# Second layer's attention weight gradients: keys' jobs first, their sets and factor loaded in the last blocks of the feed-forward gradient

## The chip, the cores and the metric

The kernel runs on one core of a Trainium2 chip. The metric is the device time of one execution in microseconds (us); lower is better. The core has five engines with a queue each: TensorE (PE, matmuls into PSUM), VectorE (DVE), ScalarE (ACT), GpSimd (POOL) and SyncE (SP), which here issues every DMA.

## What is computed

The reference runs four residual layers on 2048 tokens of width 512, two linear-attention layers (A) and two gated feed-forward layers (B), in the order A, B, A, B with shared weights, and returns the output and the gradients of the input and of the five weight matrices.

```python
def _fwd_reference(A_x, A_wqkv, A_wo, B_x, B_w_gate, B_w_up, B_w_down):
    def _A_ref(x, wqkv, wo):
        H = 32; Dh = D // H
        qkv = (x @ wqkv).reshape(B, S, 3, H, Dh) ...
        phi = lambda t: jnp.where(t > 0, t + 1, jnp.exp(t)) + 1e-6
        pq, pk = phi(q), phi(k)
        kv = jnp.einsum("bhsd,bhse->bhde", pk, v)
        z = jnp.einsum("bhsd->bhd", pk)
        num = jnp.einsum("bhqd,bhde->bhqe", pq, kv)
        den = jnp.einsum("bhqd,bhd->bhq", pq, z)[..., None] + 1e-6
        return (num / den) ... @ wo
    def _B_ref(x, w_gate, w_up, w_down):
        h = _sigmoid(x @ w_gate) * (x @ w_up)
        return h @ w_down
    x = A_x
    x = x + _A_ref(_layernorm(x), A_wqkv, A_wo)
    x = x + _B_ref(_layernorm(x), B_w_gate, B_w_up, B_w_down)
    x = x + _A_ref(_layernorm(x), A_wqkv, A_wo)
    x = x + _B_ref(_layernorm(x), B_w_gate, B_w_up, B_w_down)
    return x
...
_out, _vjp = jax.vjp(_f, A_x, A_wqkv, A_wo, B_w_gate, B_w_up, B_w_down)
```

Layers are numbered 0 to 3 in the code (A, B, A, B). The "second layer" of the title is layer 2, the second attention layer.

## The kernel before

The forward pass stores what the backward pass needs in device memory: the normalized inputs `sv_h`, for attention `sv_pk`, `sv_phq`, `sv_pqn`, for the feed-forward layers `sv_ssd`. The backward pass goes through layers 3, 2, 1, 0. The gradient of the residual stays in SBUF.

**Feed-forward gradient.** `BBwd.run` handles a B layer in four blocks B of 512 tokens, each in 11 steps u over 128 columns of the hidden width. `D(n)` multiplies the gradient by `wdT` (L1481, tile `dhh_ps`, PSUM tag "g" with two banks), ACT copies it to `dhb` (L1487), DVE and POOL multiply with the two halves of `ssd` into `dd` (L1488, L1489). `R(n)` closes a group of three columns: DVE transposes `dd` in 32 by 32 pieces into `tr_stg` (L1092; three buffers) and SP stores them as `sv_hdd` or, for the last group, `sv_hdl` (L1095). `H(B, u)` multiplies `dd` by `wuT` and `wgT` (L1513). `D` and `R` run two steps ahead of `H`. After a group's last `D` the group after next is loaded (`load_ssd`, L1461, two buffers), which the object keeps as `last_ssd`. A block ends with the layer norm's gradient, among it four operations on DVE (L1330) and ACT (L1311). `hooks` maps a place `(B, u)` to a function that is called there.

**Attention gradient.** `ABwd.first` goes through 16 row tiles `st`; for each there are TensorE's `dp_ps`, `gT_ps` and `dz_ps` and on DVE six operations (L1886, L1887, L1931, L1933, L1936, L1937). Then come `GT_ps` (L1987) and `ABwd.second`.

**Weight gradients.** These are made in `p2_gen`, a generator that is stepped between other work. One job makes a group of columns of one weight's gradient, from a set of two halves (`p_set`, two buffers each) and a factor with all 2048 tokens (`p_a` in the profile). A job has four units of 16 matmuls (L1807, `p_ps`, PSUM tag "u" with two banks), one for each 128 rows; each unit is evacuated to `dw_stg`, by ACT (L1824) if the sum over the two layers isn't finished yet and by DVE (L1822, adding the part stored before) if it is. `prefetch(i + 2)` in a job's last unit loads the set of the job after next into the buffers that this job has done with. The attention jobs are 256 columns wide. Their sets are of queries (`sv_dq`, two plain loads of 512 KB, L1673) or of keys (`sv_dkT`, four transposing loads of 256 KB, L1670), 1 MB each. Their factor is `sv_h` of the layer, loaded in four quarters of 512 KB (L1740).

**The second list of jobs, `w2`**, is opened by the hook `open_w2` at `(1, 0)` of layer 1's feed-forward gradient. It holds the four attention jobs of layer 2 in the order query, query, key, key (`a_jobs`), then twelve feed-forward jobs of layer 1 (the first is the last columns of `wd`, whose set is `sv_hdl`), then four attention jobs of layer 0. Opening it loads `MT` (`load_MT`, for the next attention gradient), the set of job 0, the factor and the set of job 1. Its units are consumed from the end of layer 1's block 3: two there, 20 in `ABwd.first` of layer 0 (one for each row tile and one more after each fourth), the rest later.

**Order of the work.** PE, ACT, DVE and POOL run in the order in which the code traces instructions (`manual_schedule(engines=EM)`). SP isn't in `EM`: a scheduler of the compiler orders its DMAs by its own estimate of when each is ready, those traced earlier first. So a load can go long before the place where the code has it, when its buffer is free; `tc.issue_after(ins)` puts what is traced in it behind `ins` on its queue.

```python
def prefetch(i):
    ...
    with k.tc.issue_after(R.pins.pop(i)) if i in R.pins else nullcontext():
        h = dict(set=(p2_set if nm == "wqkv" else p2_set_b)(k, R, *src))
```

Of the kernel before, what the change touches and what calls it, by code (L numbers as in the profile page):

```python
# [9 lines left out]
BF16 = mybir.dt.bfloat16  # L10
# [8 lines left out]
D = 512  # L19
# [3 lines left out]
P = 128  # L23
NST = S // P
# [7 lines left out]
NB = 4  # L32
GW = 256
# [32 lines left out]
def kernel(  # L66
# [22 lines left out]
    k = K()  # L89
# [20 lines left out]
    for l in range(4):  # L110
# [26 lines left out]
        wqkv=dram.tile([D, 2 * D], BF16, name="dwp_wqk"),  # L137
# [98 lines left out]
    if True:  # L236
        def load_b_weights(after):
            k.wdT = wb.tile([P, NDC, FP], BF16, name="wdT", tag="w_c")
            k.wuT = wb.tile([P, NFC, D], BF16, name="wuT", tag="w_a")
            k.wgT = wb.tile([P, NFC, D], BF16, name="wgT", tag="w_b")  # L240
            half = NFC // 2 + 1
            parts = [(k.wdT[:, c:c + 2, :], k.wT["wdT"][c * P:(c + 2) * P, :]) for c in (0, 2)]
            for t_sb, src in ((k.wuT, k.wT["wuT"]), (k.wgT, k.wT["wgT"])):
                parts += [(t_sb[:, c:e, :], src[c * P:e * P, :]) for c, e in ((0, half), (half, NFC))]
            for ins, (dst, src) in zip(after, parts):
                with tc.issue_after(ins):
                    nc.sync.dma_start(out=dst, in_=src.rearrange("(c p) j -> p c j", p=P))

        def load_MT(l):
            k.MT = k.mtp.tile([P, NDC, D], BF16, name="MT")  # L250
            nc.sync.dma_start(out=k.MT[:], in_=k.sv[l]["MT"].rearrange("(c p) j -> p c j", p=P))

        def load_a_weights(l):
            k.wqkvT = wb.tile([P, 3 * NDC, D], BF16, name="wqkvT", tag="w_a")
            woT_GT = wb.tile([P, 2, NDC, D], BF16, name="woT_GT", tag="w_b")
            k.Nv = wb.tile([P, NDC, D], BF16, name="Nv", tag="w_c")
            k.woT, k.GT = woT_GT[:, 0, :, :], woT_GT[:, 1, :, :]
            view = lambda d: d.rearrange("(c p) j -> p c j", p=P)
            yield nc.sync.dma_start(out=k.woT, in_=view(k.wT["woT"]))
            for i in (2, 0, 1):  # L260
                yield nc.sync.dma_start(out=k.wqkvT[:, i * NDC:(i + 1) * NDC, :],
                                        in_=view(k.wT["wqkvT"][i * D:(i + 1) * D, :]))
        k.load_b_weights, k.load_a_weights, k.load_MT = load_b_weights, load_a_weights, load_MT

        R = P2Res(k)
        w = {}

        def open_a1():
            k.pre["close"]()
            R.big = bctx.enter_context(tc.tile_pool(name="p2pool", bufs=1, side="right", reuse_waits="tile"))  # L270
            k.mtp = bctx.enter_context(tc.tile_pool(name="MTp", bufs=1, side="right", reuse_waits="tile"))
            k.load_MT(2)
            w["h3"] = b_load_all(k, R, k.sv[3]["h"], "p2_a1")

        def open_a2(l):
            k.a2ctx = ExitStack()
            pool = (k.a2ctx if l == 3 else bctx).enter_context(
                tc.tile_pool(name=f"a2_{l}", bufs=1, reuse_waits="tile"))

            k.a2 = pool.tile([P, NST, D], BF16, name="p2_a2")  # L280
            k.load_a2 = lambda b: b_load_batch(k, R, k.a2, k.sv[l]["gbf"], b)

        def open_sets():
            R.sets = bctx.enter_context(tc.tile_pool(name="p2sets", bufs=2, side="right", reuse_waits="tile"))
            R.stage = bctx.enter_context(tc.tile_pool(name="p2stage", bufs=2, side="right", reuse_waits="tile"))
            R.pins = dict(enumerate(B3.ssd_dmas[-2:]))
            w[3] = Units(p2_gen(k, R, b_jobs(k, 3, lambda: w["h3"])), b_units())
            return w[3]

        def open_w2():  # L290
            k.load_MT(0)
            jobs = a_jobs(k, 2, once(lambda: a_load_all(k, R, k.sv[2]["h"], "p2_a1")))
            jobs += b_jobs(k, 1, lambda: w["h1"]) + a_jobs(k, 0, lambda: w["h0"])
            w[2] = Units(p2_gen(k, R, jobs), len(jobs) * NDC)
            return w[2]

        def load_h1(b):
            if b == 0:
                w["h1"] = R.big.tile([P, NST, D], BF16, name="p2_a1")
            b_load_batch(k, R, w["h1"], k.sv[1]["h"], b)  # L300
        k.load_h1 = load_h1

        A2, A0 = ABwd(k, R, 2), ABwd(k, R, 0, out1)
        B3.run(A2, {(1, 8): open_a1, (3, 5): open_sets})
        open_a2(3)
        w3 = w[3]
        A2.first(w3)
        A2.second(w3)
        w3.take(w3.left - 4)
        k.a2ctx.close()  # L310
        BBwd(k, 1).run(A0, {(1, 0): open_w2}, rest=w3)
        open_a2(1)
        R.stage_a = bctx.enter_context(tc.tile_pool(name="p2stage_a", bufs=2, reuse_waits="tile"))
        w2 = w[2]
        A0.first(w2)
        A0.second(w2)
        tail = bctx.enter_context(tc.tile_pool(name="t_big", bufs=1, reuse_waits="tile"))
        last = 2 * D // GW * NDC
        w["h0"] = tail.tile([P, NST, D], BF16, name="t_a1")
        for b in range(NST // NB):  # L320
            w2.take(NDC)
            R.tail = tail
            with tc.issue_after(R.last_set):
                a_load_batch(k, R, w["h0"], k.sv[0]["h"], b)
        T = {}
        loads = a_small_loads(k, tail, T)
        for i in range(w2.left - last):
            next(w2)
            with tc.issue_after(R.last_set):
                next(loads, None)  # L330
        drain(loads)
        sg = a_small_grads(k, tail, T)
        for i in range(last):
            if i == last - 1:
                next(sg, None)
            next(w2)
            if i % 2 == 1 and i < last - 1:
                next(sg, None)
        drain(w2)
        drain(sg)  # L340
# [52 lines left out]
def dram_batch(ap2d, b, nb=NB):  # L393
    return ap2d[batch_rows(b, nb), :].rearrange("(n p) d -> p n d", p=P)
# [1236 lines left out]
def drain(gen):  # L1631
    for _ in gen:
        pass


class Units:

    def __init__(self, gen, n):
        self.gen, self.left = gen, n
        self.R = next(gen)  # L1640

    def __iter__(self):
        return self

# [9 lines left out]
def b_units():  # L1654
    return 3 * (NG + 1) * NDC
# [45 lines left out]
def b_jobs(k, l, h):  # L1701
    sv, nms, final = k.sv[l], ("wd", "wu", "wg"), l == 1
    wd = [(0, g) for g in range(NG + 1)]
    if final:
        order = wd[NG:] + wd[:NG] + [(i, g) for g in range(NG + 1) for i in (1, 2)]
    else:
        order = [(i, g) for g in (0, NG, 1) for i in (1, 2)] + [wd[g] for g in (0, NG, 1, 2)] + [(1, 2), (2, 2)]
    return [(nms[i], (sv, i, g), CG[g][0] * P, XG if g < NG else F - NG * XG, final, h if i else lambda: k.a2)
            for i, g in order]


def a_jobs(k, l, h):
    n = D // GW
    return [("wqkv", (k.sv[l], g // n, g % n), g * GW, GW, l == 0, h) for g in range(2 * n)]


def once(f):
    got = []

    def get():  # L1720
        if not got:
            got.append(f())
        return got[0]
    return get


def b_load_batch(k, R, t, src, b):
    R.eng().dma_start(out=t[:, b * NB:(b + 1) * NB, :].rearrange("p (n e) d -> p n e d", e=2),
                      in_=src[batch_rows(b), :].rearrange("(n p e) d -> p n e d", p=P, e=2))


def b_load_all(k, R, src, name, pool=None):
    t = (pool or R.big).tile([P, NST, D], BF16, name=name)
    for b in range(NST // NB):
        b_load_batch(k, R, t, src, b)
    return t


def a_load_batch(k, R, t, src, b):
    R.eng().dma_start(out=t[:, b * NB:(b + 1) * NB, :], in_=dram_batch(src, b))  # L1740


def a_load_all(k, R, src, name):
    t = R.big.tile([P, NST, D], BF16, name=name)
    for b in range(NST // NB):
        a_load_batch(k, R, t, src, b)
    return t


def p2_gen(k, R, jobs):  # L1750
# [41 lines left out]
        return [lambda j0=j0: part(j0) for j0 in range(0, n, 2)]  # L1792

    prefetch(0)
    jobs[0][5]()
    prefetch(1)
    yield R
    for i, (nm, src, c0, w, final, factor) in enumerate(jobs):
        h = held.pop(i)
        set_t = h["set"]  # L1800
# [422 lines left out]
```

## Time and profile before

| what | us |
|---|---|
| median of 3 runs | 1098.92 (1098.82 to 1100.64) |
| profiled execution | 1098.47 |
| its span, first to last instruction | 1096.8 |
| layer 1's feed-forward gradient, blocks 0 to 3 | about 709 to 824 in the span |
| layer 0's `ABwd.first`, row tiles with `w2` units | about 824 to 885 |
| layer 0's GT and `ABwd.second` | about 885 to 965 |
| remaining units of `w2` | about 965 to 1094 |

Busy shares of the span are TensorE 98%, VectorE 65%, ScalarE 44%, GpSimd 42%; the mean granted TensorE clock is 1.000. The DMA queue moved 268.81 MB, taking 86.5% of the 16 engines' span.

How to read the lines below: times within the span are in us from its start. In a waits row, the numbers are the total us waited, how often, and the longest. In a timeline row, they are start and duration in us, engine, line, operation, the tiles as out<-in, and, in brackets, idle time just before and what ended it. In a windows row each engine has its busy us and the number of its instructions in the stretch.

### The profile page before, as it was taken

What the parts mean: (1) busy time and instruction counts of PE and PEld (TensorE: products, weight loads), DVE (VectorE), ACT (ScalarE), POOL (GpSimd) and SP (SyncE); (2) the same over time, 40 slices, a digit from 0 to 9 for tenths busy, and PEclk for the clock granted to TensorE, in tenths of its full rate; (3) what the DMA queues carried; (4) which work ended last, traced back from release to release, by engine and by line L of the source; (5) the groups of instructions that cost most, each with busy time, mean ns of one, the idle gap of its engine ahead of it and who ended that gap; (6) DMA issues with size and microseconds to landing.
All of it is one profiled execution on the core that took longest, in us unless ns stands there. A gap on an engine that the chain in (4) does not pass through costs nothing. (4 is left out here: it accounts for less than half of the span.)

```text
span 1096.8 us, 19853 instructions
## 1 busy us (share of the span) xinstructions
PE 1076.1 (98%) x7239; PEld 660.6 (60%) x7340; DVE 718.2 (65%) x1257; ACT 483.2 (44%) x905; POOL 464.1 (42%) x631
## 2 busy tenths in 40 slices
PE   8999999999999999999999999999999999999998
PEld 4467777547777744445756556544447755555587
DVE  7798997878888677777965630067778946632221
ACT  6676555647555524445633441234346513420001
POOL 5738776425765447773101420048871102410000
PEclk9999999999999999999999999999999999999999
DMA  8948997895797688875899978998869999968997
GB/s 252 321 156 213 253 248 240 225 247 154 213 296 231 188 271 292 297 254 194 250 256 272 252 233 281 289 318 261 233 189 240 281 247 281 249 201 272 257 273 169
DMA packets 383202, 270.08 MB, mean 246 GB/s; under 512 B 134976, under 2 KB 368896, under 8 KB 383104
## 3 DMA queue, kind: packets, MB, share of 16 engines
q1 hardware_dynamic: 383104, 268.81, 86.5%
q8 instruction: 57, 0.93, 0.3%
q14 instruction: 41, 0.34, 0.1%
HBM read 122.62 MB, written 119.47 MB: 221 GB/s over the span
## 5 line engine op out<-in xcount | busy, mean ns | idle before, releaser
L1807 PE MATMUL p_ps<-p_set,p_a 128*128 128x384 bf16 (+2 forms) x1792 | 264.7, 303 | 2.0 <-DVE dw_stg L1822 0.7
L1807 PEld LDWEIGHTS <-p_a 128*128 128x128 bf16 x1792 | 168.8, 96 | 86.2 <-issue 2.0
L1489 POOL TENSOR_TENSOR dd<-dhb,ssd 128x512 bf16<-128x512 bf16 x84 | 96.9, 1158 | 101.5 <-ACT dhb L1487 94.3
L1488 DVE TENSOR_TENSOR dd<-dhh_ps,ssd 128x512 bf16<-128x512 f32 x85 | 57.2, 679 | 118.7 <-ACT dhb L1487 114.9
L1513 PE MATMUL dh_ps<-wuT,dd 128*128 128x512 bf16 (+1 forms) x339 | 128.5, 379 | 0.5
L1513 PE MATMUL dh_ps<-wgT,dd 128*128 128x512 bf16 (+1 forms) x329 | 124.7, 379 | 0.1
L1513 PEld LDWEIGHTS <-dd 128*128 128x128 bf16 x680 | 66.3, 98 | 79.8 <-POOL dd L1489 0.4
L1154 POOL TENSOR_TENSOR ssd_t<-hhT,oms 128x512 bf16<-128x512 bf16 (+2 forms) x76 | 83.9, 1112 | 45.6 <-DVE hhT L1153 18.2
L1822 DVE TENSOR_TENSOR dw_stg<-p_ps,dw_stg 128x384 bf16<-128x384 f32 (+2 forms) x76 | 32.0, 438 | 105.4 <-PE p_ps L1807 95.9
L1487 ACT CAST dhb<-dhh_ps 128x512 bf16<-128x512 f32 x84 | 48.7, 589 | 114.7 <-PE dhh_ps L1481 106.9
L1135 PE MATMUL g_ps<-hT,wg 128*128 128x256 bf16 (+1 forms) x792 | 92.8, 261 | 0.7 <-DVE den L974 0.4
L1135 PE MATMUL u_ps<-hT,wu 128*128 128x256 bf16 (+1 forms) x792 | 92.8, 261 | 0.0
L1092 DVE STREAM_TRANSPOSE tr_stg<-dd 128x768 f32<-128x768 f32 (+1 forms) x62 | 86.9, 1437 | 4.7 <-DMA sv_hdd<-tr_stg 3.6
L1135 PEld LDWEIGHTS <-wg 128*128 128x128 bf16 x792 | 70.0, 98 | 16.9 <-issue 0.5
L1170 PE MATMUL y_ps<-wd,hhT 128*128 128x512 bf16 (+1 forms) x337 | 77.9, 379 | 0.8
L1481 PE MATMUL dhh_ps<-gT,wdT 128*128 128x512 bf16 x299 | 76.7, 379 | 1.7 <-DVE dd L1488 0.9
L1135 PEld LDWEIGHTS <-wu 128*128 128x128 bf16 x792 | 70.6, 98 | 7.4 <-issue 0.4
L1151 ACT ACTIVATE ssd_t<-g_ps 128x512 bf16<-128x512 f32 (+2 forms) x76 | 42.5, 559 | 61.7 <-PE g_ps L1135 54.1
L1824 ACT CAST dw_stg<-p_ps 128x384 bf16<-128x384 f32 (+2 forms) x76 | 28.1, 386 | 85.3 <-PE p_ps L1807 81.5
L1481 PEld LDWEIGHTS <-wdT 128*128 128x128 bf16 x352 | 34.3, 98 | 42.5 <-issue 2.7
L1152 ACT ACTIVATE oms<-g_ps 128x512 bf16<-128x512 f32 (+2 forms) x96 | 53.7, 559 | 10.9 <-POOL ssd_t L1154 9.9
L1153 DVE TENSOR_TENSOR hhT<-u_ps,ssd_t 128x512 bf16<-128x512 f32 (+2 forms) x76 | 47.3, 630 | 16.8 <-PE u_ps L1135 9.1
(259 smaller groups left out, 1878.4 us busy)
## 6 DMA issues: line engine op xcount, KB each, us to landing
sv_hdd<-tr_stg SPq DMA_DIRECT2D x72, 384.0 KB, 4.7
p_set<-sv_hdd SPq DMA_DIRECT2D x36, 768.0 KB, 6.4
ssd<-sv_ssd SPq DMA_DIRECT2D x23, 768.0 KB, 5.2
sv_ssd<-ssd_t SPq DMA_DIRECT2D x61, 256.0 KB, 3.5
h_ld<-sv_h SPq DMA_DIRECT2D x30, 256.0 KB, 4.1
sv_hdl<-tr_stg SPq DMA_DIRECT2D x24, 256.0 KB, 4.8
p_a<-sv_h SPq DMA_DIRECT2D x12, 512.0 KB, 6.6
p_set<-sv_hdl SPq DMA_DIRECT2D x24, 256.0 KB, 4.7
```

The costliest lines, as they stand in the source:

```text
L1092: nc.vector.transpose(t[:, :, 0:n * P].bitcast(F32).rearrange("p q (a j) -> p q a j", a=2 * n), src.rearrange("p c x -> p (c x)").bitcast( ...
L1135: nc.tensor.matmul(ps[:, ci * n:(ci + 1) * n], lhsT=w_sb[:, kc, (c0 + ci) * P:(c0 + ci + 1) * P], rhs=hT[:, kc, (st % 2) * P:(st % 2) * P ...
L1152: nc.scalar.activation(oms, gv, ACT.Sigmoid, scale=-1.0)
L1153: nc.vector.tensor_tensor(hh, uv, ssd[:, :, 0, :], ALU.mult)
L1154: nc.gpsimd.tensor_tensor(ssd[:, :, 1, :], hh, oms, ALU.mult)
L1170: nc.tensor.matmul(y_ps[:], lhsT=h[0:r, fc, off:off + P], rhs=k.wd[0:r, fc, :], start=(fc == 0), stop=(fc == NFC - 1))
L1481: nc.tensor.matmul(ps[:], lhsT=k.wdT[:, jc, u * P:(u + 1) * P], rhs=self.gT[B][:, jc, :], start=(jc == 0), stop=(jc == NDC - 1))
L1487: nc.scalar.copy(dhb[:], ps[:])
L1488: nc.vector.tensor_tensor(self.dd[ng][:, 0, c, :], ps[:], self.ssd[ng][:, c, 0, :], ALU.mult)
L1489: nc.gpsimd.tensor_tensor(self.dd[ng][:, 1, c, :], dhb[:], self.ssd[ng][:, c, 1, :], ALU.mult)
L1513: nc.tensor.matmul(self.acc[j][:], lhsT=dd[0:r, a, c, j * P:(j + 1) * P], rhs=w[0:r, u, :], start=(u == 0 and a == 0), stop=(u == NFC - 1 ...
L1807: nc.tensor.matmul(ps[:, 0:w], lhsT=lhs[:, s, ic * P:(ic + 1) * P], rhs=rhs, start=(s == 0), stop=(s == NST - 1))
```

## The change

Two things are changed for `w2`. The four attention jobs of layer 2 come in the order key, key, query, query (groups 2, 3, 0, 1). And what `open_w2` loaded at once is spread over hooks in layer 1's feed-forward gradient: `MT` at `(1, 2)`; the four quarters of the factor at `(2, 1)`, `(2, 4)`, `(2, 7)` and `(2, 10)`; the first keys' set at `(3, 2)`, with the opening of the list; the second keys' set at `(3, 5)`. All but `MT` are put behind the latest `ssd` load on SP's queue. `p2_gen` now stops once after its first prefetch and once after its second; `Units.ahead` steps it from the one to the other, and the earlier list `w3` calls it right away. `w2` then loads its queries' sets by `prefetch(2)` and `prefetch(3)`.

```diff
             w[3] = Units(p2_gen(k, R, b_jobs(k, 3, lambda: w["h3"])), b_units())
+            w[3].ahead()
             return w[3]
 
+        def load_h2(b):
+            if b == 0:
+                w["h2"] = R.big.tile([P, NST, D], BF16, name="p2_a1")
+            with tc.issue_after(B1.last_ssd):
+                a_load_batch(k, R, w["h2"], k.sv[2]["h"], b)
+
         def open_w2():
-            k.load_MT(0)
-            jobs = a_jobs(k, 2, once(lambda: a_load_all(k, R, k.sv[2]["h"], "p2_a1")))
+            jobs = a_jobs(k, 2, lambda: w["h2"], (2, 3, 0, 1))
             jobs += b_jobs(k, 1, lambda: w["h1"]) + a_jobs(k, 0, lambda: w["h0"])
+            R.pins[0] = B1.last_ssd
             w[2] = Units(p2_gen(k, R, jobs), len(jobs) * NDC)
             return w[2]
+
+        def more_w2():
+            R.pins[1] = B1.last_ssd
+            w[2].ahead()
...
-        BBwd(k, 1).run(A0, {(1, 0): open_w2}, rest=w3)
+        B1 = BBwd(k, 1)
+        B1.run(A0, {(1, 2): lambda: k.load_MT(0), (2, 1): lambda: load_h2(0), (2, 4): lambda: load_h2(1),
+                    (2, 7): lambda: load_h2(2), (2, 10): lambda: load_h2(3), (3, 2): open_w2, (3, 5): more_w2},
+               rest=w3)
...
+    def ahead(self):
+
+        next(self.gen)
+
...
-def a_jobs(k, l, h):
+def a_jobs(k, l, h, order=range(2 * D // GW)):
     n = D // GW
-    return [("wqkv", (k.sv[l], g // n, g % n), g * GW, GW, l == 0, h) for g in range(2 * n)]
-
-
-def once(f):
...
+    return [("wqkv", (k.sv[l], g // n, g % n), g * GW, GW, l == 0, h) for g in order]
...
-def a_load_all(k, R, src, name):
...
     prefetch(0)
-    jobs[0][5]()
+    yield R
     prefetch(1)
-    yield R
+    yield
     for i, (nm, src, c0, w, final, factor) in enumerate(jobs):
```

More of the change, by code (lines that the diff above doesn't have):

```diff
@@ L1709, in b_jobs @@
             for i, g in order]
-def a_jobs(k, l, h):
+def a_jobs(k, l, h, order=range(2 * D // GW)):
     n = D // GW
-    return [("wqkv", (k.sv[l], g // n, g % n), g * GW, GW, l == 0, h) for g in range(2 * n)]
-def once(f):
[L1718 to L1724, printed above, removed]
+    return [("wqkv", (k.sv[l], g // n, g % n), g * GW, GW, l == 0, h) for g in order]
 def b_load_batch(k, R, t, src, b):
@@ L1740, in a_load_batch @@
     R.eng().dma_start(out=t[:, b * NB:(b + 1) * NB, :], in_=dram_batch(src, b))
-def a_load_all(k, R, src, name):
[L1744 to L1747, printed above, removed]
 def p2_gen(k, R, jobs):
```

## The prediction

> **What bounds the kernel now.** I read the page's busy times first, then the waits of TensorE from 700 to 890 us (the only part in which the change touches anything), then the busy time by stage, then the queues of SP and VectorE around each wait.
>
> ```profile
> span 1096.8 us, 19853 instructions
> PE 1076.1 (98%) x7239; PEld 660.6 (60%) x7340; DVE 718.2 (65%) x1257; ACT 483.2 (44%) x905; POOL 464.1 (42%) x631
> ...
> PE dhh_ps L1481 <- DVE dd L1488: 0.7, 1, 0.7
> PE p_ps L1807 <- DMA p_set<-sv_hdl: 0.6, 2, 0.3
> PE p_ps L1807 <- DVE dw_stg L1822: 0.3, 1, 0.3
> PE p_ps L1807 <- DMA p_set<-sv_dkT: 0.2, 1, 0.2
> ```
>
> TensorE is busy 98% of the span, and between 700 and 890 us it waits 1.8 us in five places. These waits count from the modelled end of a matmul, which overlaps the next one; what they cost is read from the starts instead: a 512-column matmul starts every 0.216 us, a 256-column one every 0.109 us. In starts the losses are 0.82 us at 742.6 (the DVE wait), 0.39 at 857.6 (dkT), about 1.0 around 868 to 869 (hdl) and 0.45 at 881.7 (dw_stg): 2.7 us. No edit of loads can give back much more than that. The stages, in the windows view (us, PE, PEld, DVE, ACT, POOL busy, clock, DMA share, GB/s):
>
> ```profile
> 709.00:741.00 32.00, 31.84 (x146) 14.38 (x148) 21.20 (x25) 13.21 (x27) 14.19 (x14) 1.00 1.05 314
> 741.00:770.00 29.00, 28.24 (x130) 12.81 (x131) 21.50 (x30) 13.74 (x28) 23.08 (x24) 1.00 0.89 262
> 770.00:799.00 29.00, 28.75 (x132) 13.00 (x134) 21.61 (x28) 12.13 (x24) 23.11 (x24) 1.00 0.79 231
> 799.00:824.00 25.00, 24.80 (x117) 11.37 (x118) 18.01 (x20) 9.65 (x17) 21.27 (x19) 1.00 0.59 179
> 824.00:855.00 31.00, 30.74 (x273) 24.46 (x276) 28.21 (x56) 19.10 (x44) 4.98 (x11) 1.00 0.97 238
> 855.00:885.00 30.00, 28.69 (x256) 21.13 (x259) 28.45 (x63) 12.86 (x26) 4.67 (x9) 1.00 0.99 293
> ```
>
> The first four rows are blocks 0 to 3 of the feed-forward gradient, the last two the attention stage's first half. The DMA engines are full in block 0 and idle most in block 3. In the last two rows VectorE is busy 56.7 of 61 us, and its timeline shows why that matters: from 829.07 to 887.65 us it never stands idle but once.
>
> ```profile
> 869.96 0.42 DVE L1937 TENSOR_TENSOR phq_ld<-t_t,phq_ld 128x512 bf16<-128x512 bf16 x1
> 870.30 0.45 DVE L1822 TENSOR_TENSOR dw_stg<-p_ps,dw_stg 128x128 bf16<-128x128 f32 x2
> 871.06 0.42 DVE L1886 TENSOR_TENSOR prod<-dp,pqn 128x512 bf16<-128x512 bf16 x1 [0.31 <-ACT dp L1878]
> ...
> 881.19 0.45 DVE L1822 TENSOR_TENSOR dw_stg<-p_ps,dw_stg 128x128 bf16<-128x128 f32 x2
> ```
>
> The 0.31 us at 871 is that idle time. The last line is the evacuation that TensorE waits for at 881.70.
>
> **Part 1: what leaves block 0.** Before, the two query sets and h of layer 2 are issued as soon as their buffers come free, in the SP timeline at 704 to 726 us: four set loads and four of p_a, 512 KB each, landing 1.4 to 1.8 us apart, so some 12 us of DMA time in a stage whose share is 1.05. The damage is a late store: VectorE wants a third tr_stg buffer at 735.1 and gets it at 737.02.
>
> ```profile
> 725.52 1.16 SPq L1673 DMA_DIRECT2D p_set<-sv_dq  x1
> 729.35 0.33 SPq L1461 DMA_DIRECT2D ssd<-sv_ssd  x1
> 730.44 1.97 SPq L1095 DMA_DIRECT2D sv_hdd<-tr_stg  x2
> ...
> 737.02 1.11 DVE L1092 STREAM_TRANSPOSE tr_stg<-dd 128x512 f32<-128x512 f32 x1 [1.89 <-DMA sv_hdd<-tr_stg]
> ```
>
> That makes the block's four L1330 operations late, then L1488, then a PSUM bank: 0.82 us. Blocks 1 and 2 lose 0.25 us at the same place (771.4, 800.1) with shorter store waits (1.39 and 0.35 us). So I take block 0 to come down to their level: **-0.57 us**; bounds 0 (the gT transposes at 732 to 741 alone keep the store late) and -0.82.
>
> **Part 2: the attention stage.** Jobs 0 and 1 now find both sets in place, and jobs 2 and 3 load query sets by two plain transfers each instead of four transposes. Before, SP spends 7.28 us at 835.43 and 5.58 + 1.27 us at 847.58 on the eight transposes, 14.1 us; four L1673 issues, at 0.37 to 1.16 us in block 0, are 1.5 to 4.6 us. SP is then some 6 us ahead when the hdl set of job 4 can go (job 2 ends at 854.6; it went at 859.05 and landed at 868.95, wanted at 866.8). The waits of 0.39 and 1.0 us go. But that does not reach the end: job 4's and 5's evacuations sit in VectorE's queue behind the row tiles' work, and the 22nd unit (a quarter of a job, 16 matmuls; the 384-column one at 881.70) needs that of the 20th. VectorE can be earlier only by its idle 0.31 us. So 1.4 us of DMA wait become a longer dw_stg wait: gain **-0.3 us**, not -1.4; bounds 0 and -1.85 (0.39 + 1.0 + 0.45, if nothing on VectorE holds it).
>
> **Part 3: what blocks 2 and 3 get.** The four quarters of h go in block 2 behind the ssd loads at 773.23, 780.27, 787.29 and 792.45, each 0.8 to 1.1 us of SP (the p_a issues at 709 to 718) and 1.4 us of DMA time; at a share of 0.79, 5.6 us over 29 makes 0.98. Behind each in the queue are two hdd or hdl stores, whose landing frees tr_stg. The tightest is the store issued at 788.39, landed 793.31, for the transpose that already waits 0.35 us at 793.40: 1.4 us later it ends at 796.4, against 796.1 where L1330 starts today for ACT's sake. Cost 0 to 0.3, **+0.15**.
>
> The eight key transposes go in block 3 behind the ssd loads at 801.98 and 809.02. Each was 1.23 to 3.27 us on SP, and landed about 1.0 us after the one before (853.25, 854.19, 855.17), 256 KB each. What they can hold up are the two hdd stores after either ssd load:
>
> ```profile
> 801.98 0.33 SPq L1461 DMA_DIRECT2D ssd<-sv_ssd  x1
> 802.40 1.85 SPq L1095 DMA_DIRECT2D sv_hdd<-tr_stg  x2
> 809.02 0.33 SPq L1461 DMA_DIRECT2D ssd<-sv_ssd  x1
> 809.44 1.89 SPq L1095 DMA_DIRECT2D sv_hdd<-tr_stg  x2
> ```
>
> The first store landed at 808.26, and VectorE needs its buffer at 809.2. SP is not ordered by hand: a ready instruction traced earlier goes first. The stores are traced before the hooks and get ready within 2 us of the ssd load, so at most one or two transposes should slip ahead of each, as before at 847.58, where three went, then two dq stores that had become ready, then the fourth. One or two transposes ahead: landing 809.6 to 810.6, a stall of 0.4 to 1.4 us on VectorE, in a stretch where dd is needed 5.2 us after its matmul begins and is ready after 2.2: absorbed. I take **+0.1**, bounds 0 and +3.75 (second rival). h_ld moves from 811 to about 817 and is wanted at 824.3; SP has the time, busy 7 us of 22 in this stretch, plus 10 to 15.
>
> All of these go on SP's queue; POOL's and ACT's carry none of them. At no cost: the MT load, which went at 562.6 us when its buffer came free and still can; the removed `once` and the factor call, which issue nothing new; the earlier weight gradients' generator, whose two prefetches go in the same order.
>
> **Sum:** -0.57 - 0.3 + 0.15 + 0.1 = -0.6 us. Profiled execution: 1098.47 us, span 1096.8 and 1.7 around it; it lies 0.45 under the median 1098.92. So 1097.9 for its like, **1098.3 us** as a median. Own range 1097.5 to 1099.6.
>
> **Rivals.** *Everything comes back.* For: all five waits have DMA or its delays behind them. Against: VectorE's unbroken row. It needs VectorE's operations themselves to begin earlier. Worth 0.57 + 0.39 + 1.0 + 0.45 = 2.4 us: 1096.5.
>
> *The key transposes shut out block 3's stores.* All four issue in a row behind the ssd load, as at 835.43 (7.28 us). The first store then goes at 809.7, lands at about 812.3 behind four landings at 1.0, and VectorE, wanting the buffer at 809.2, stalls 3.1 us; the D matmul due at 813.2 needs a bank that dd frees at 814.45 instead of 811.4: 1.25 us. The second four push the next store to 819 and its landing to 822.5, against 818.3: 4.2 us, of which the last chunks' matmuls see about 2.5. With block 2's 0.3 and less 0.87 gained: 1098.92 + 3.75 + 0.3 - 0.87 = 1102.1. It decides as soon as a store that was ready leaves more than about 3 us late. For: the run of four at 835.43. Against: nothing earlier in trace order was ready then. [...]
>
> *Relief and cost cancel.* Block 0 keeps its store wait (gT transposes), block 2 and 3 lose 0.4: 1099.0.
>
> **How the numbers follow.** A measurement of this kernel can tell about 0.2%, 2.2 us, from no change. Forecast 0.50, all back 0.18, stores shut out 0.22, cancel 0.10. Faster than 1096.7: 0.18 and 0.02 of the forecast's tail, 0.20; slower than 1101.1: 0.22 and 0.02, 0.24; within: 0.56. The range reaches to both outer cases, 1096.2 to 1102.2.
>
> **What would show it.** Right: no p_set wait before 870 us and one dw_stg wait of 1 us or more near 881; tr_stg waits near 736 under 1.4 us; the bank wait at 742 down to 0.25 or gone; stores of block 3 between transposes. Wrong: the dw_stg wait gone or small while the stage is shorter by over a microsecond (then VectorE was no cap), or tr_stg waits over 2 us after 809 with PE idle at dhh_ps behind them.

## The result, and the profile after

The changed kernel is slower: a median of 1101.74 us (8 runs, 1100.68 to 1103.54) against 1098.86 us (8 runs, 1097.34 to 1100.64) for the kernel before on the same chip. The ratio is 1.0029, with a 95% interval of 1.0019 to 1.0038, so 2.9 us by the medians: a small change, but clear of the interval. The profiled execution took 1100.68 us with a span of 1099.0, against 1098.47 and 1096.8. From here on, lines of the changed kernel are up to 15 higher than those of the kernel before (L1095 is L1109, L1330 is L1344, L1488 is L1502, L1807 is L1808).

The waits view of TensorE over the same stretch, 690 to 900 us, after the change (total us, times, longest):

```profile
PE p_ps L1808 <- DVE junk L1344: 1.8, 1, 1.8
PE dh_ps L1527 <- DVE dd L1502: 1.1, 1, 1.1
PE p_ps L1808 <- DMA p_set<-sv_hdl: 0.9, 2, 0.6
PE dhh_ps L1495 <- DVE dd L1502: 0.7, 2, 0.4
PE p_ps L1808 <- DMA p_set<-sv_dq: 0.3, 1, 0.3
PE p_ps L1808 <- DVE dw_stg L1823: 0.3, 1, 0.3
PE dh_ps L1527 <- DVE junk L1344: 0.2, 1, 0.2
```

The two largest are new, and both name VectorE. Read from the starts of matmuls, what is lost beyond the usual spacing is: 0.27 us at 741.35 (block 0's end, 0.82 before), 0.40 at 770.2 (block 1's end, 0.25 before), 0.34 and 0.61 at 798 to 800 (block 2's end, 0.25 before), **1.31 at 821.7 and 1.93 at 831.9** (block 3 and its layer norm, nothing before), 0.49 at 849.4 (a set of queries; a set of keys cost 0.39 before), 0.81 and 0.42 at 871 to 872 (hdl; 0.46 and 0.46 before), 0.44 at 884.7 (dw_stg, as before). That is 7.0 us against 3.1, 3.9 more. This execution was ahead by then for reasons that lie before the change's stretch: block 0's wait ended at 741.35 against 742.62, 1.27 us earlier, and only 0.55 of that is the shorter wait (at 670 us, TensorE was 0.84 ahead already). Without the other 0.72 the last unit beside the row tiles should begin 3.2 us later; it began at 884.71 against 881.70, 3.0 later. The span is only 2.2 us longer, since the execution before lost another 0.61 us at 1058.9, to a wait for dw_stg that the one after doesn't have.

Why VectorE is late is in SP's timeline of block 3, after the change (start, duration, line, operation, tiles, count):

```profile
801.55 0.35 SPq L1475 DMA_DIRECT2D ssd<-sv_ssd  x1
801.95 1.89 SPq L1109 DMA_DIRECT2D sv_hdd<-tr_stg  x2
803.89 0.70 SPq L1748 DMA_DIRECT2D p_a<-sv_h  x1
804.64 7.95 SPq L1688 DMA_TRANSPOSE p_set<-sv_dkT  x4
812.71 0.51 SPq L1475 DMA_DIRECT2D ssd<-sv_ssd  x1
813.32 1.23 SPq L1109 DMA_DIRECT2D sv_hdd<-tr_stg  x2
814.60 8.44 SPq L1688 DMA_TRANSPOSE p_set<-sv_dkT  x4
823.13 1.22 SPq L1109 DMA_DIRECT2D sv_hdd<-tr_stg  x2
824.44 1.94 SPq L1480 DMA_DIRECT2D h_ld<-sv_h  x2
826.47 1.44 SPq L1109 DMA_DIRECT2D sv_hdl<-tr_stg  x2
829.94 1.17 SPq L1915 DMA_DIRECT2D phq_ld<-sv_phq  x2
```

Each set of keys goes as four transposes in one unbroken row, 8.0 and 8.4 us of SP. Everything behind them is late: the second ssd load 3.7 us (809.02 before), the two stores behind it 3.9 (809.44), the next two 6.0 (817.12), h_ld 13.0 (811.42), phq_ld 5.5 (824.48). Between 801.55 and 827.91 SP spends 23.8 of 26.4 us on issuing; before, between 801.9 and 824.4, it spent 5.8 of 22.5.

VectorE's timeline shows what that does (idle time just before, and what ended it, in brackets):

```profile
815.09 1.58 DVE L1106 STREAM_TRANSPOSE tr_stg<-dd 128x768 f32<-128x768 f32 x1
819.49 1.58 DVE L1106 STREAM_TRANSPOSE tr_stg<-dd 128x768 f32<-128x768 f32 x1 [2.82 <-DMA sv_hdd<-tr_stg]
...
826.27 1.09 DVE L1106 STREAM_TRANSPOSE tr_stg<-dd 128x512 f32<-128x512 f32 x1 [2.90 <-DMA sv_hdd<-tr_stg]
828.51 0.75 DVE L1344 SCALAR_TENSOR_TENSOR junk<-dh_ps,rstd_all,h_ld 128x512 bf16<-128x512 f32 x1 [1.15 <-DMA h_ld<-sv_h]
```

Three waits in a row: for the store issued at 813.32 (landed 819.39), for the one at 823.13 (landed 826.17), and then for h_ld. The first of these stores was issued at 809.44 before and landed at 813.96. It landed 5.4 us later, then, 3.9 of them because SP issued it later and 1.6 because it took longer from issue to landing (6.08 against 4.52 us). `junk` began at 824.27 before and begins at 828.51 now. The last of these four layer norm operations ends at 831.84 against 829.15: 2.7 us late at the door of the stage in which VectorE has no time to spare. In that stage, 824 to 885, the windows view has TensorE and VectorE so (columns as in the prediction):

```profile
799.00:824.00 25.00, 23.41 (x112) 10.52 (x110) 16.65 (x19) 8.72 (x15) 21.23 (x19) 1.00 0.91 219
824.00:855.00 31.00, 28.91 (x254) 22.12 (x252) 26.66 (x52) 18.66 (x42) 4.37 (x10) 1.00 0.90 266
855.00:885.00 30.00, 28.81 (x266) 22.01 (x265) 28.12 (x62) 14.28 (x29) 4.73 (x9) 1.00 0.98 291
```

Block 3's DMA share went from 0.59 to 0.91, by half, and its GB/s from 179 to 219, by a fifth. VectorE stands idle once after 831.84, 0.72 us at 874, where it waits for `dp` behind TensorE's late hdl set (0.31 at 871 before). Its lateness is 2.7 us at 831, 2.6 at 858 and 3.0 after that wait. TensorE came out of block 3 late as well, by its own loss of 3.2 us, so this trace alone doesn't tell which of the two engines carries the delay to the end.

### The profile page after: what moved, and what is told of

It reads as the page before. It is cut to its first block, busy times and chain, and to the rows that moved or that the text cites. A ratio compares the mean times of both kernels' runs of the same rounds, so it can differ in the third digit from the quotient of the medians.

```text
span 1099.0 us, 19948 instructions
## 1 busy us (share of the span) xinstructions
PE 1081.0 (98%) x7340; PEld 660.7 (60%) x7340; DVE 719.7 (65%) x1257; ACT 483.2 (44%) x905; POOL 462.0 (42%) x631
## 5 line engine op out<-in xcount | busy, mean ns | idle before, releaser
L1808 PE MATMUL p_ps<-p_set,p_a 128*128 128x384 bf16 (+2 forms) x1792 | 264.3, 303 | 3.3 <-DVE junk L1344 1.8
L1808 PEld LDWEIGHTS <-p_a 128*128 128x128 bf16 x1792 | 168.9, 96 | 87.0 <-issue 3.7
L1502 DVE TENSOR_TENSOR dd<-dhh_ps,ssd 128x512 bf16<-128x512 f32 x85 | 57.0, 678 | 116.9 <-ACT dhb L1501 113.8
L1527 PE MATMUL dh_ps<-wgT,dd 128*128 128x512 bf16 (+1 forms) x340 | 128.8, 379 | 0.0
L1184 PE MATMUL y_ps<-wd,hhT 128*128 128x512 bf16 (+1 forms) x352 | 81.1, 379 | 0.0
L1167 DVE TENSOR_TENSOR hhT<-u_ps,ssd_t 128x512 bf16<-128x512 f32 (+2 forms) x76 | 47.3, 630 | 16.4 <-PE u_ps L1149 9.5
```

The costliest lines, as they stand in the source:

```text
L1167: nc.vector.tensor_tensor(hh, uv, ssd[:, :, 0, :], ALU.mult)
L1184: nc.tensor.matmul(y_ps[:], lhsT=h[0:r, fc, off:off + P], rhs=k.wd[0:r, fc, :], start=(fc == 0), stop=(fc == NFC - 1))
L1502: nc.vector.tensor_tensor(self.dd[ng][:, 0, c, :], ps[:], self.ssd[ng][:, c, 0, :], ALU.mult)
L1527: nc.tensor.matmul(self.acc[j][:], lhsT=dd[0:r, a, c, j * P:(j + 1) * P], rhs=w[0:r, u, :], start=(u == 0 and a == 0), stop=(u == NFC - 1 ...
L1808: nc.tensor.matmul(ps[:, 0:w], lhsT=lhs[:, s, ic * P:(ic + 1) * P], rhs=rhs, start=(s == 0), stop=(s == NST - 1))
```

## The experiments

The theory after this reading: SP's time in two unbroken rows of transposes makes block 3's stores and loads late. Its rivals were the bytes that block 3 moves now, h_ld alone, the factor's quarters in block 2, and that VectorE's stage would be late whatever is loaded where. In the expectations A stands for SP's time and D for the bytes. Each ratio is to the kernel before on the same chip, with its 95% interval; absolute times of different chips aren't compared.

### The order alone

The kernel before, with only the order of layer 2's four jobs changed; everything is still loaded at `(1, 0)`.

```diff
-    return [... for g in range(2 * n)]
+    return [... for g in ((2, 3, 0, 1) if l == 2 else range(2 * n))]
```

> The kernel before with the keys' jobs first and nothing else: all loads stay where they were, in block 0. Theory A (in the changed kernel two runs of four transposes on SP's queue in block 3 hold up that block's stores and h_ld, VectorE begins the layer norm and the attention stage 2.7 us late, and that stage, which VectorE fills, carries the delay to its end): the order by itself does no harm, 1097.9 to 1099.2; the dkT wait at 857 gone, a dw_stg wait near 881 of 0.5 us or more in its place, no dhh or junk wait in block 3. Theory B (the loss is made in the attention stage by the new order of jobs, whose dq and hdl sets still come late there): 1100.5 or more.

Measured: 1100.70 us against 1098.99, ratio 1.0016 (1.0006 to 1.0026). TensorE's waits from 690 to 900 us:

```profile
PE dhh_ps L1481 <- DVE dd L1488: 1.7, 2, 1.2
PE p_ps L1807 <- DVE dw_stg L1822: 1.1, 2, 0.7
PE dh_ps L1513 <- DVE junk L1330: 0.3, 1, 0.3
```

Not one wait for a set is left, and the wait for dw_stg has grown instead. In starts it is 0.57 and 0.84, 1.41 us, where the kernel before lost 1.75 to sets and dw_stg together. That is the cap of the prediction's Part 2, and its size: -0.34 us. The total missed the expectation, and the trace shows a reason: the eight transposes now go ahead of block 0 and in it (six in a row from 703.25, two at 726.49) and do there what they do in block 3 of the changed kernel. VectorE waits 3.85 us for a tr_stg buffer at 738.7, and TensorE loses 2.66 us between 740.4 and 744.3 (2.4 and 3.1 in the two kernels below that use this order too).

### The factor's quarters alone

The four quarters of h in block 2 as in the changed kernel, `MT` at `(1, 2)`; old order, the sets at the old place `(1, 0)`.

```diff
-            jobs = a_jobs(k, 2, once(lambda: a_load_all(k, R, k.sv[2]["h"], "p2_a1")))
+            jobs = a_jobs(k, 2, lambda: w["h2"])
...
+            w[2].ahead()
...
+        B1.run(A0, {(1, 0): open_w2, (1, 2): lambda: k.load_MT(0), (2, 1): lambda: load_h2(0), ...
```

> The changed kernel's four late quarters of h alone; jobs in the old order, both queries' sets loaded at the old place in block 0. Theory A: block 0's bank wait at 742 goes from 0.82 to 0.3 us, blocks 2 and 3 lose 0.3 to 0.6 at their start, so 1098.5 to 1099.3. Theory C (it is the added DMA work of h in blocks 2 and 3, behind which stores and h_ld come late, that costs): 1100.5 or more, with a wait of TensorE for junk after block 3.

Measured: 1097.71 us, ratio 0.9993 (0.9984 to 1.0003), the lowest ratio of the kernels that leave nothing out. Block 0's end loses 0.27 us (0.82 before), block 1's 0.47, block 2's 0.26; 0.95 us go to a set of keys, 0.70 to hdl and 0.43 to dw_stg. So block 0 does as Part 1 said, the quarters cost block 2 nothing in this execution, and they aren't what made the kernel slower.

### The same bytes without transposes

The changed kernel with the old order of jobs: the sets in block 3, at the same places and of the same size, are queries', two plain loads each.

```diff
-            jobs = a_jobs(k, 2, lambda: w["h2"], (2, 3, 0, 1))
+            jobs = a_jobs(k, 2, lambda: w["h2"])
```

> The changed kernel with the old order of jobs: at the same two places in block 3 the same bytes are loaded, by two plain transfers each (about 1 us of SP each) in place of four transposes (8.0 and 8.3 us of SP). Theory A (SP's time is what holds up the stores): block 3's VectorE waits for tr_stg fall from 2.8 and 2.9 us to under 1 and 1, the 1.9 us wait for junk goes, 1098.7 to 1099.7. Theory D (the transfer of 2 MB more in block 3 is what delays the stores' landing, whoever issues it): 1101 or more.

Measured: 1098.06 us, ratio 1.0002 (0.9991 to 1.0013). SP in block 3:

```profile
803.61 3.09 SPq L1691 DMA_DIRECT2D p_set<-sv_dq  x2
807.50 1.50 SPq L1475 DMA_DIRECT2D ssd<-sv_ssd  x1
809.10 1.21 SPq L1109 DMA_DIRECT2D sv_hdd<-tr_stg  x2
810.36 3.49 SPq L1691 DMA_DIRECT2D p_set<-sv_dq  x2
815.62 1.98 SPq L1109 DMA_DIRECT2D sv_hdd<-tr_stg  x2
817.69 1.43 SPq L1480 DMA_DIRECT2D h_ld<-sv_h  x2
```

A set of the same 1 MB takes 3.1 to 3.5 us of SP instead of 8.0 to 8.4. The second pair of stores goes at 809.10 and the third at 815.62, h_ld at 817.69. VectorE's longest wait for a tr_stg buffer is 1.1 us, TensorE loses nothing in block 3, and the slowdown is gone. It is therefore the transposes and not the bytes. The landings say how. The store issued at 809.10 landed at 815.08, after 5.98 us, about as long as in the changed kernel (6.08), so the longer way from issue to landing goes with the bytes, and VectorE absorbs it here: its transpose at 815.50 waits for nothing. What differs is the issue: counted from block 3's first D matmul (800.10, 798.60 and 799.67), SP issues this store after 9.3 us in the kernel before, 10.5 here and 13.7 in the changed kernel. What stays is what the kernel before has too: waits for a set of keys (1.05 us), hdl (0.73) and dw_stg (0.43).

### One transpose at a time

The keys stay first, but their eight transposes are spread: one each at `(1,1)`, `(1,4)`, `(1,7)`, `(1,9)`, `(3,1)` and `(3,4)`, two behind the second h_ld; quarters of h at `(2,1)`, `(2,4)`, `(2,7)`, `(2,9)`.

```diff
+        for i, u in enumerate((1, 4, 7, 9)):
+            hooks[1, u] = lambda i=i: key(i)
+            hooks[2, u] = lambda i=i: load_h2(i)
+        hooks[3, 1] = lambda: key(4)
+        hooks[3, 4] = lambda: key(5)
```

> The changed kernel with its eight transposes one at a time: four in block 1 and two in block 3, each behind one ssd load, two behind block 3's h_ld; the last quarter of h a place earlier. Theory A: no run of transposes, so no store of block 3 over 3 us late; the waits of 1.3 and 1.9 us at the end of block 3 go to under 0.5 together, VectorE begins the layer norm's last part within 0.5 us of the kernel before; 1097.8 to 1099.2. If transposes cost wherever they are (theory E): 1100.5 or more.

Measured: 1099.18 us, ratio 1.0003 (0.9995 to 1.0012). In block 3 one transpose (2.87 and 1.75 us of SP) stands ahead of each ssd load or h_ld, the stores go at 810.83 and 818.64, and TensorE loses nothing. But the four in block 1 do harm: there the next stores wait, VectorE stands 2.90 us for a buffer at 766.3, and block 1's end loses 1.67 us; block 2's end loses 1.13. The attention stage's waits are dw_stg (1.0) and hdl (0.32). (Block 2's end loses as much in kernels that load nothing new there, as shown further down.) So the interleaving that the prediction assumed is harmless in block 3, when it is made by hand, and not in block 1, where `gT` has transposes of its own (two at 770.31, 3.36 us of SP).

### Only the second set out of the way

The changed kernel, with the second set of keys put behind block 3's second h_ld.

```diff
         def more_w2():
-            R.pins[1] = B1.last_ssd
+            R.pins[1] = B1.last_h
...
-                    ... (3, 2): open_w2, (3, 5): more_w2},
+                    ... (3, 2): open_w2, (3, 9): more_w2},
```

> The changed kernel with its second keys' set put behind block 3's h_ld in place of the last ssd load. The first set still goes as a run of four behind its ssd load. Theory A (each run holds up the stores behind it, and each has its own wait): VectorE's wait of 2.8 us for tr_stg at 819 and TensorE's 1.3 us at 822 stay, VectorE's wait for h_ld goes, and the 1.9 us wait for junk falls to 0.3 to 1.0; 1099.6 to 1101. Theory F (h_ld is all that matters): as the kernel before or better, 1098.9 or less.

Measured: 1101.12 us, ratio 1.0013 (1.0003 to 1.0024). The wait for h_ld is gone, and the 1.93 us loss at 831.9 with it; but the wait behind the first row has grown.

```profile
820.99 1.56 DVE L1106 STREAM_TRANSPOSE tr_stg<-dd 128x768 f32<-128x768 f32 x1 [4.49 <-DMA sv_hdd<-tr_stg]
825.51 1.11 DVE L1106 STREAM_TRANSPOSE tr_stg<-dd 128x512 f32<-128x512 f32 x1 [0.67 <-DMA sv_hdd<-tr_stg]
```

The store went at 813.24, as in the changed kernel (813.32), yet landed at 820.89 instead of 819.39, with h_ld close behind it on the queue; TensorE lost 2.95 us at 823.2. One row of four is enough to cost three microseconds there. That the first wait would stay at its 1.3 us of TensorE time was wrong, and why this store's landing moved isn't settled.

### h_ld ahead of the keys

The changed kernel with block 3's two h_ld loads issued at steps 0 and 5 instead of 7 and 8 (three buffers).

```diff
-                    if u in (7, 8):
-                        self.load_h(B, u - 7)
+                    late_h = end and not self.first
+                    if u in ((0, 5) if late_h else (7, 8)):
+                        self.load_h(B, u // 5 if late_h else u - 7)
```

> The changed kernel with block 3's two h_ld ahead of both runs of transposes (a third h_ld buffer); the runs stay. Theory A (the stores behind the runs are the larger part, h_ld the smaller): the tr_stg waits of 2.8 and 2.9 us stay, the layer norm begins some 1.1 us sooner, which is VectorE's wait for h_ld: 1100.2 to 1101.3. Theory F: 1099.5 or less.

Measured: 1101.94 us, ratio 1.0027 (1.0017 to 1.0038): no gain on the changed kernel. The wait for h_ld is gone, but VectorE still waits 2.49 and 3.40 us for tr_stg, and TensorE loses 0.99 and 1.17 behind that, at block 2's end 1.9, and 0.50 and 0.85 for dw_stg. h_ld's lateness alone isn't the cause. The stretch from block 3 on did get 1.9 us shorter in this execution (see the table below), and block 2's end lost about as much; why the median gained nothing is open.

### VectorE's cap: the adds moved to other engines

Two kernels test whether VectorE's operations set the attention stage's end. At the end of layer 1's block 3, eight additions (two for each of four row tiles, 0.75 us each, 6 us of VectorE) go to POOL and ACT; once on the kernel before, once with the order changed as well.

```diff
             for x in lns:
-                x.add()
+                if self.first:
+                    x.add()
+                else:
+                    x.add_t()
+                    x.make_r()
+                    x.add_r()
```

> The kernel with the order of jobs alone, and with the eight layer norm operations at the end of layer 1's block 3 (5.4 us of VectorE) moved to GpSimd and ScalarE. The order alone has no wait for a set from 824 to 885 us but 1.4 us of waits for dw_stg. Theory G (VectorE is full in that stage, so set waits that go only turn into waits for dw_stg): the 1.4 us go, 1.0 to 1.6 us less than the order alone, 1099.1 to 1099.7. If VectorE is no cap: no change from the order alone within 0.4.

> The kernel before with the same eight operations moved to GpSimd and ScalarE. Theory G: the wait of 0.45 us for dw_stg goes, the waits for the dkT and hdl sets, about 1.4 us, stay: 0.2 to 0.6 us less than before, so less than half of what the move gives where the sets are in time. If VectorE is no cap: no change.

Measured: 1112.3 us, ratio 1.0124 (1.0107 to 1.0141), and 1110.89, ratio 1.011 (1.0094 to 1.0126). The experiment failed: ACT's `make_r` waits for POOL's `add_t` (1.26 us each, and after each POOL waits 0.92 to 0.93 us for ACT), and ACT, which takes its work in the traced order, has the copies of `g`, `gT` and `dp` behind it. TensorE stood still for 10.5 us in both (10.51 and 10.50), until ACT's `g`. Nothing on the cap can be read from this.

### VectorE's cap: the adds left out

> The kernel before without the eight layer norm operations on VectorE (5.4 us) at the end of layer 1's block 3; it leaves out the update of four row tiles of the gradient. Theory G (VectorE is full in the attention stage's first half): TensorE's 0.45 us wait for dw_stg goes, its waits for the dkT and hdl sets, about 1.4 us, stay; 0.2 to 0.7 us less than before, 1098.3 to 1098.8.

> The order of jobs alone (every set in time), without the same eight operations. Theory G: the 1.4 us of waits for dw_stg go and nothing takes their place, 1.0 to 1.8 us less than the order alone, 1098.9 to 1099.7, with block 0's losses of 2.4 us as they were. If VectorE is no cap: 1100.4 or more.

```diff
-            for x in lns:
-                x.add()
+            if self.first:
+                for x in lns:
+                    x.add()
```

These two kernels leave out the update of four row tiles of the gradient, so they are here for their times alone. Measured, on another chip whose median for the kernel before was 1099.95: without the adds 1099.21, ratio 0.9992 (0.9984 to 1.0001); with the order changed and without them 1100.60, ratio 1.0003 (0.9994 to 1.0013). The latter against 1.0016 for the order alone is 0.13%, 1.4 us. Its waits, to be held against those of the order alone:

```profile
PE dhh_ps L1481 <- DVE dd L1488: 3.2, 6, 1.1
PE dh_ps L1513 <- DVE junk L1330: 0.5, 2, 0.3
PE p_ps L1808 <- DVE dw_stg L1823: 0.3, 1, 0.3
```

With VectorE 6 us ahead, the dw_stg waits fall from 1.41 us in starts to 0.44, and there is no wait for a set: the 1.75 us of the kernel before become 0.44. Where the sets are late, relief on VectorE gives nothing in the stage: 1.70 us of waits for sets remain there (1.31 before), and 0.44 for dw_stg, which the expectation said would go; the 0.08% of the median is within the interval of no change. So both limits lie close together, and either alone gives little. The 0.44 that stays has its reason in the timeline: relieved, VectorE stands idle again and again in the stage, waiting for `dp` (with the order four times, 4.7 us in all), and for the last time at 873.97 (with the order) or 871.30 (without). From there on it needs 3.49 us for a row tile and TensorE 2.76, so it falls behind once more and the last evacuation is late, however far ahead VectorE was before. The intervals of 1.0016 and 1.0003 overlap and are from two chips, and this profiled execution (1101.67 us, above its median) lost more in the blocks than the other; what carries the reading is the waits in the stage itself.

### Half the adds, and a mixed version

On the kernel with late quarters, two of the four row tiles' adds go to ACT (into a tile of its own) and POOL; then the same with the order query, key, query, key, the first query set at its old place and the first key set's transposes one at a time in block 3.

```diff
-            for x in lns:
+            for x in lns[:0 if self.first else 2]:
+                x.add_apart(self.p["work"])
+            for x in lns[0 if self.first else 2:]:
                 x.add()
```

> The late quarters of h alone, and four of the eight layer norm operations taken off VectorE (2.7 us): two row tiles' sums are made by ScalarE into a tile of its own and two additions on GpSimd. Theory G: the wait for dw_stg (0.43) goes, the waits for the dkT and hdl sets (1.65) stay or grow a little; 0.2 to 0.6 us less than the late quarters alone: 1097.1 to 1097.6. If ScalarE's two more operations hold up TensorE, as they did when all were moved: 1098 or more.

> h's quarters late; jobs in the order query, key, query, key; the first query set at its old place in block 0, the first key set in block 3 with its four transposes one at a time (behind each ssd load and two behind h_ld); four of the eight layer norm operations off VectorE. Theory A: no wait in block 3, no wait over 0.3 us for a set before the hdl set. Theory G: with VectorE relieved the set waits that go are gained. Together 1096.2 to 1097.3, faster than both kernels. If a single transpose behind an ssd load already holds up the stores: 1098.5 or more.

```diff
+            jobs = a_jobs(k, 2, lambda: w["h2"], (0, 2, 1, 3))
...
+        hooks[3, 1] = lambda: key(0)
+        hooks[3, 4] = lambda: key(1)
```

Measured: 1100.73, ratio 1.0013 (1.0002 to 1.0023), and 1098.93, ratio 0.9994 (0.9986 to 1.0003). Both missed what was expected of them. The mixed version has no loss in block 3, no wait for a set ahead of hdl's (0.32 and 0.43) and dw_stg waits of 0.63 and 0.85: still capped. But these two kernels are no test of the cap, because moving the adds didn't relieve VectorE. The first row is from the kernel before, the others from the mixed version:

```profile
829.85 0.75 DVE L1324 SCALAR_TENSOR_TENSOR x<-t_sb,ab,x 128x512 f32<-128x512 f32 x1
...
829.16 1.80 DVE L1355 SCALAR_TENSOR_TENSOR x<-t_sb,ab,x 128x512 f32<-128x512 f32 x1
830.49 1.49 POOL L1363 TENSOR_TENSOR x<-x,dhb 128x512 f32<-128x512 f32 x1
834.12 1.37 DVE L1916 TENSOR_TENSOR prod<-dp,pqn 128x512 bf16<-128x512 bf16 x1
```

While POOL makes its four additions, VectorE's own additions take 1.64 to 1.80 us each instead of 0.75, and `prod` 1.37 instead of 0.42. From the last `junk` to the end of the first `prod`, VectorE needs 7.0 us with half the adds and 6.1 with all of them. In the first kernel the pqn load ahead of the keys on SP's queue went 1.0 us later than with the quarters alone, counted from the start of block 3, and the last transpose landed 1.2 later; that is about the size by which the wait for keys grew, to 2.03 us at 859.1. The link to VectorE's slower start is likely and not tested. The mixed version is clearly better than the changed kernel, and neither it nor the quarters alone is clearly better than the kernel before.

### One stretch in every kernel

Blocks 0 to 2 lose different amounts from one execution to the next, as Part 1 and block 2 below show. So the stretch that matters is set side by side here: from block 3's first D matmul (800.10 before, 799.67 after) to the start of the second 384-column unit (881.70, 884.71), in the profiled executions.

| kernel | us |
|---|---|
| before | 81.6 |
| changed | 85.0 |
| order alone | 81.2 |
| factor's quarters alone | 81.8 |
| plain loads in place of transposes | 82.0 |
| one transpose at a time | 81.1 |
| second set behind h_ld | 85.0 |
| h_ld ahead of the keys | 83.2 |
| adds left out; with the order too | 81.9; 80.2 |
| half adds; mixed | 83.1; 82.0 |

The three kernels with four transposes in a row in block 3 are the slowest of these, with the first half-adds kernel next to them. Even one row costs the whole 3.4 us where h_ld isn't ahead of it. Only the order together with VectorE's relief is more than 0.6 us under the kernel before.

## Why the prediction was wrong

**Part 1 gave the right end value, with less of a gain than it seems.** Block 0's bank wait fell from 0.82 to 0.27 us (0.25 forecast), and it is 0.25 to 0.27 in all eight profiled executions in which h is out of block 0. But with all loads in place the same end of block 0 lost 0.82 in the kernel before, 0.27 with the adds moved and 1.74 with the adds left out, and neither of these two edits touches block 0. So the 0.82 from which the -0.57 was taken was one draw of a wide spread.

**Part 3 is the step that failed**, in "at most one or two transposes should slip ahead of each" and so in the **+0.1** taken from bounds of 0 to +3.75. All four transposes of each set went in a row, twice. The reason given, that stores traced earlier and ready within 2 us would go first, doesn't hold: VectorE had filled the first store's buffer by 808.89, and SP began transposes at 809.94 and 811.29 before it issued that store at 813.32; in the second row three transposes went ahead of a store that was ready at 816.67. SP's order comes from a scheduler in the compiler that goes by its own estimate of when a DMA is ready; that this estimate put the transposes first fits the trace, but the estimate itself isn't on record. The profile had a row that spoke for this (7.28 us of SP at 835.43), and the prediction set it aside because nothing earlier in trace order was ready then. What the runs show in place of +0.1 is 3.24 us of TensorE time in block 3 and its layer norm. Plain loads of the same size at the same places cost nothing there. The waits of 2.82 and 2.90 us for tr_stg are the second sign of being wrong that the prediction named, and TensorE stood idle behind them, though at dh_ps and p_ps and not at dhh_ps.

**"h_ld moves from 811 to about 817"** was wrong by 7 us, and "10 to 15" for eight transposes too: they took 16.4 us, the first of each row 3.0 and 3.8. h_ld went at 824.44 and ended up as the last of the three waits. The loads of the attention stage behind it started late as well.

**Block 2's +0.15** can't be checked. Its end lost 0.95 us against 0.25 before. But with the quarters in block 2 the profiled executions range from 0.25 to 1.9, and without them from 0.26 to 1.8 (0.26 with the order alone, 1.0 with the adds left out, 1.6 with the adds moved). What the quarters cost there is less than this spread.

**Part 2's mechanism was right, its use one-sided.** VectorE does cap the stage: with the sets in time, dw_stg takes most of what the sets gave back, -0.34 us where -0.3 was forecast. In the changed kernel that never came into play. The sentence "SP is then some 6 us ahead" failed, since SP came into the stage late and the four query loads took 6.2 us of it where 1.5 to 4.6 were assumed, and waits of 0.49 for a query set and 1.23 us for hdl stand where 0.39 and 0.92 stood: 0.4 us lost in place of 0.3 gained. And I used VectorE's unbroken row only to cut the gain: an engine without idle time also passes on a late start (2.7 us at 831, 2.6 at 858).

**The second rival was what happened**, at 1102.1 for a measured 1101.74. It had the first row's length (7.28 us for 7.95) and the first stall (3.1 us for 2.82) right, and 1.25 us of TensorE time for 1.31. Its second stall was thought to reach the last chunks' matmuls with 2.5 us; the runs put it at VectorE's transpose and at h_ld, which the rival had left out, and 1.93 us at the first p_ps unit. So the mechanism was right, while the closeness of the totals is partly luck: the second stall was priced 0.6 us too high, and the 0.3 us credited to Part 2 was not gained.

That rival let the stores land behind the transposes ahead of them on the queue, which was the author's estimate. In the changed kernel the first row's transposes landed from 811.09 to 814.83, the ssd load behind them at 818.32 and the store at 819.39, and in both profiled executions, before and after, all 807 transfers landed in the order of their issue. The landings, which that rival spaced at 1.0 us, came 1.28, 1.49 and 0.97 us after one another in the first row and 1.14, 1.50 and 0.97 in the second: 768 KB in 3.74 and 3.61 us, which is 210 and 218 GB/s. The second plain load of 512 KB in the queries' version landed 1.76 us after the first, 298 GB/s, and the two that the changed kernel issues at 838.12 and 839.38 landed 1.72 us apart, 305 GB/s. In these rows SP issues a transpose only every 1.35 us or more, so the issue may set the spacing of the landings, and no run here tells the two apart.

**The chances.** The second rival had 0.22. Two rows of the profile, four transposes in one go and 1.23 to 3.27 us for each, gave a length near 8 us against a slack of 3; the interleaving that should have prevented it had been seen once, at 847.58, and there too three transposes had gone in a row first.

## What to carry to other kernels

Cost a load that is moved by the time that its issue takes on its queue, not by its bytes alone: here 1 MB is 8 us of SP as four transposes and 3.1 to 3.5 us as two plain loads, and all that is traced near it on that queue waits for the whole row. Tying a load "behind X" says nothing of what it goes ahead of; where stores free the buffers of a busy engine, break such a row up and put it where their slack is longest. An engine without idle time over a stage is read both ways: it swallows what waits elsewhere give back (1.75 us of waits became 1.41 of another here), and it hands on a late start (2.6 of 2.7 us). And before work is moved off it, look at how long its other operations take beside the moved ones: here they took twice as long (1.64 to 1.80 us for 0.75).

## What else the runs showed of the hardware

In the changed kernel the first transposes of a row take longest on SP: 3.04, 2.17, 1.30, 1.30 us and 3.78, 1.91, 1.30, 1.30. In the kernel before it is the second: 1.26, 3.27, 1.25, 1.30. So 1.25 to 1.30 us is the least that one of 256 KB took there; what the longer ones wait for isn't in the trace.

In the kernel with the adds moved (without the order), TensorE's timeline after its standstill reads:

```profile
842.98 0.61 PE L1872 MATMUL gT_ps<-ident,g 128*128 128x128 bf16 x4 [10.50 <-ACT g L1864]
843.38 3.62 PE L1812 MATMUL p_ps<-p_set,p_a 128*128 128x256 bf16 x16
...
848.28 1.91 PE L1812 MATMUL p_ps<-p_set,p_a 128*128 128x256 bf16 x16
```

The same sixteen matmuls of 256 columns take 3.62 us and five microseconds later 1.91: 0.213 us from start to start against 0.109. The slow stretch lasts from 842.98 to 847.63. In the kernel with the order changed too, the sixteen behind a standstill of 10.51 us take 3.62 us as well, and the next sixteen 1.91. The mean granted clock of these two executions is 0.995, against 1.000 in the profiled execution before. After the changed kernel's waits of 1.14 and 1.76 us (821.70 and 831.90) the matmuls start at the full rate, every 0.216 and 0.109 us; from what length on a standstill is followed by the slow rate, no run here shows. An estimate from these times: half of the 4.7 us of the slow stretch, some 2.3, is what this standstill cost on top of itself.
